# Two attention layers in one fixed order for four engines, value matmuls in query halves, 45 score tiles' exponentials on VectorE

## Chip, core and metric

The kernel runs on one core of a Trainium2 chip. The metric is device time in microseconds. The engines are called PE (TensorE), DVE (VectorE), ACT (ScalarE), POOL (GpSimd) and SP (SyncE, which issues DMAs).

## What is computed

Four layers run one after the other on x of 2048 tokens by 512 channels, 32 heads of 16: softmax attention (A), linear attention with a learned feature map (B), A and B again, each behind a layer norm and with a residual. The weights of both A layers are the same, and so are those of both B layers.

```python
def _A_ref(x, wqkv, wo):
    ...
    scores = jnp.einsum("bhqd,bhkd->bhqk", q, k) * (Dh ** -0.5)
    p = _softmax(scores, axis=-1)
    o = jnp.einsum("bhqk,bhkd->bhqd", p, v)
    return (lambda x, *d: x.transpose(*d))(o, 0, 2, 1, 3).reshape(B, S, D) @ wo
...
x = A_x
x = x + _A_ref(_layernorm(x, axis=-1), A_wqkv, A_wo)
x = x + _B_ref(_layernorm(x, axis=-1), B_wqkv, B_w_phi, B_wo)
x = x + _A_ref(_layernorm(x, axis=-1), A_wqkv, A_wo)
x = x + _B_ref(_layernorm(x, axis=-1), B_wqkv, B_w_phi, B_wo)
```

Matmul operands that are not FP32 are split into a high and a low FP16 part, so a projection is three passes.

## The kernel before

`LayerA.attention` is what the change rewrites. A layer's 32 heads are four octets `o` of eight heads. An octet has two groups `g` of four heads, and each group runs over four query blocks `j` of 512 and 16 key tiles `kt` of 128: 8 x 4 x 16 = 512 steps `n` a layer. A step has two score tiles (`half` 0 and 1, two heads each). `scores` (L944) computes one: eight matmuls into a PSUM tile `s` of 128 keys by 2 x 512 queries (there are two such tiles, four banks in all), then one ACT instruction that writes the exponentials to a tile `p` in SBUF (there are six). A row of `kq`, written with the shift, keeps the exponent in range, so no maximum is taken. `pvs` (L954) multiplies a step's two `p` tiles with the values `v`, FP32, eight matmuls of 512 columns, summed over the 16 key tiles in a PSUM pair `double`. After the last key tile `norm` (L554) turns the pair on DVE (`turned_sum`: two transposes `yt` on DVE, their sum on POOL), divides by the row sums on DVE, and with the second group of an octet `finish_o` writes the result `osp` and SP stores it to `oD`.

The rest of the layer is side work on PE between these, kept in the list `fill`. `octet(o)` projects the next octet's values (`pv`, turned like `yt` and stored in `v` by 16 DMAs, L726) and its queries and keys (`pqk`, L643); DVE scales and clamps them from PSUM into `stg` (`tq`, L821 to L826), POOL squares them, and SP loads `kq` from `stg` with 12 DMAs a group. `part(j)` multiplies three octets' output with `wo` (`po`) and DVE adds it to x (L626); `tail(j)` does the fourth and the next layer norm. In the first A layer `prep_b` folds `w_phi` into B's weights, and `prep_rest` loads the other weights, takes their largest element on DVE (`peaks`, L325) and splits them (`split_parts`, L145, L148). Side results go to a second PSUM pair, called by its use (`pv`, `pqk`, `po`, `psn`).

What sets the order: PE's is written by hand. The loop in `attention` puts half 1 of step n, then the value matmuls of step n - 1 or side work, then half 0 of step n + 1, and a credit of 1.45 to 1.75 side units a step says how much side work goes in:

```python
with tc.manual_schedule(engines={E.PE}):
    self.scores(*order[0], 0)
    for n, (g, j, kt) in enumerate(order):
        ...
        credit = min(credit + rate(n), 6)
        self.scores(g, j, kt, 1)
        turn = bool(pend) and pend[0][2] == 0 and not owed
        if turn:
            credit = sides(n, 3, credit, True)
        elif pend:
            self.pvs(*pend.popleft())
```

A pause of two or three steps (`GAP`, `hold`) after each side result is meant for DVE to empty the pair. The order on DVE, ACT and POOL is that of a list scheduler in the recording layer, which places instructions when the program is built. Each engine then runs its instructions in that order and waits on semaphores. SP's order comes from the same scheduler, before and after the change. The B layers and the stretch between layers are the same in both kernels but for line numbers, one added one-element operation where the shift is computed, and the place of a few rows where a layer ends.

## Time and profile before

| | us |
|---|---|
| three timed runs | 2669.97, 2670.04, 2676.82 |
| median | 2670.04 |
| the profiled execution | 2663.27 |
| its span, first to last instruction | 2661.4 |
| granted PE clock, mean | 0.974 |

The profile is one execution. A row of its groups names the source line, the engine, the operation and the tiles (out<-in), the shape and count, then busy time, the mean of one, and the idle time of the engine just before with what ended it. A row of the timeline has start and length in us and in brackets the idle time before it. Busy time counts overlapping instructions once. The lines that matter stand with the argument below.

### The profile page before, as it was taken

The numbers are of one execution on the slowest core, as the hardware profiler recorded it, in microseconds if no ns is written. First come the engines' busy times: TensorE is split into PE (matmuls) and PEld (weight loads), VectorE is DVE, ScalarE is ACT, GpSimd is POOL, SyncE is SP. The second block draws the span as 40 slices with busy tenths as digits, with TensorE's granted clock in tenths as the row PEclk, the third lists the DMA queues.
The fourth block names the chain that finished last, engine by engine and source line by source line (L and its number), as shares of the span: only waits on it lengthen the run. The fifth ranks groups of instructions, "written<-read, shape, count | busy, mean of one in ns | idle before, by whom it ended". The sixth has DMA issues, their size and how long they took to land.

```text
span 2661.4 us, 102775 instructions
## 1 busy us (share of the span) xinstructions
PE 2351.9 (88%) x46698; PEld 1100.2 (41%) x46698; DVE 1165.2 (44%) x2143; ACT 2194.4 (82%) x2426; POOL 486.5 (18%) x607
## 2 busy tenths in 40 slices
PE   7889998999888898899788899989998898888998
PEld 4444444444443343345344444444443344434543
DVE  8123222223333346599861233222232221557897
ACT  5899999999998798554438999999999899985453
POOL 3111110111100000266440111111111000004652
PEclk8999999999999999999899999999999999999999
DMA  5300320231035311000233003203300441110003
GB/s 197 70 13 7 56 38 3 40 66 35 18 78 142 141 69 66 17 25 1 76 101 53 15 7 51 39 3 49 61 3 11 94 118 50 58 58 21 13 17 105
DMA packets 111049, 138.62 MB, mean 52 GB/s; under 512 B 64025, under 2 KB 65673, under 8 KB 108425
## 3 DMA queue, kind: packets, MB, share of 16 engines
q1 hardware_dynamic: 109416, 129.18, 19.7%
q8 instruction: 367, 6.01, 0.9%
q0 software_dynamic: 1184, 2.77, 0.3%
q14 instruction: 82, 0.66, 0.1%
HBM read 60.06 MB, written 39.85 MB: 38 GB/s over the span
## 4 chain that ended last, share of the span: by engine, by line
ACT 47%; PE 18%; DVE 17%; issue 11%; POOL 3%; SPq 2%; DMA 1%; ACTq 0%; DVEq 0%; POOLq 0%
ACT p L951 45%; PE double L965 5%; PE s L948 3%; DVE su L1224 2%; DVE xt L626 1%; DVE yt L549 1%; POOL yt L550 1%; PE pbv L1154 1%; PE po L637 1%; PE pk L1154 1%; PE po L643 1%; SPq L726 1%; PE pq L1154 1%; POOL f L1233 1%; DVE st L432 1%
## 5 line engine op out<-in xcount | busy, mean ns | idle before, releaser
L951 ACT ACTIVATE p<-s 128x1024 f32<-128x1024 f32 x2048 | 1911.9, 1055 | 117.7 <-PE s L948 109.2
L965 PE MATMUL double<-p,v 64*32 64x512 f32 x16384 | 1117.9, 598 | 6.1 <-DVE yt L549 3.2
L948 PE MATMUL s<-kq 49*32 49x512 f16 x15488 | 828.5, 384 | 139.9 <-ACT p L951 112.9
L948 PEld LDWEIGHTS <-kq 49*32 49x32 f16 x15872 | 384.4, 90 | 898.9 <-issue 813.5
L965 PEld LDWEIGHTS double<-p,v 64*32 64x32 f32 x16384 | 320.6, 107 | 93.9 <-issue 30.4
L550 POOL TENSOR_TENSOR yt<-yt,yt 128x512 f32<-128x512 f32 x64 | 81.6, 1276 | 956.7 <-DVE yt L549 908.4
L549 DVE STREAM_TRANSPOSE yt<-double 128x512 f32<-128x512 f32 x128 | 84.2, 695 | 374.7 <-PE double L965 374.2
L821 DVE TENSOR_SCALAR tq<-pqk,c_qk 128x512 f32<-128x512 f32 x48 | 35.7, 744 | 342.6 <-PE pqk L643 330.0
L626 DVE SCALAR_TENSOR_TENSOR xt<-po,c_oA,xt 128x512 f32<-128x512 f32 x120 | 89.1, 743 | 219.9 <-PE po L643 214.3
L1154 PEld LDWEIGHTS <-xnTa 128*128 128x128 f16 x1152 | 111.2, 99 | 157.2 <-DVE f L1217 29.5
L744 POOL TENSOR_TENSOR sq<-stg 128x512 bf16<-128x512 f16 x48 | 58.2, 1212 | 498.9 <-DVE stg L823 389.7
L1233 POOL TENSOR_TENSOR f<-f,su 128x1024 f32<-128x1024 f32 x62 | 119.8, 1933 | 140.0 <-DVE su L1227 105.3
L549 DVE STREAM_TRANSPOSE vyt<-pv 128x512 f32<-128x512 f32 x48 | 31.9, 695 | 217.0 <-PE pv L643 216.7
L643 PE MATMUL po<-woA,ob 64*32 64x512 f16 x2304 | 100.2, 380 | 24.1 <-DVE xt L626 24.1
L1218 ACT ACTIVATE f<-f,c_pB 128x1024 f32<-128x1024 f32 x64 | 72.6, 1148 | 52.0 <-DVE f L1217 51.9
L1154 PE MATMUL pbv<-wbv,xnTa 128*128 128x512 f16 x384 | 93.1, 395 | 24.7 <-DVE f L1217 24.7
L643 PEld LDWEIGHTS <-wA 64*32 64x32 f16 x4608 | 77.7, 93 | 73.3 <-issue 39.6
L643 PE MATMUL pqk<-xnTb,wA 64*32 64x512 f16 x2304 | 96.4, 377 | 10.9 <-DVE tq L821 7.0
L643 PE MATMUL pqk<-xnT,wA 64*32 64x512 f16 x2304 | 95.1, 378 | 11.9 <-DVE tq L821 5.9
L1239 ACT ACTIVATE fk<-f 128x1024 f16<-128x1024 f32 x30 | 31.7, 1057 | 73.5 <-POOL f L1233 73.5
L1154 PE MATMUL pq<-wbqk,xnTa 128*128 128x512 f16 x384 | 88.4, 379 | 0.0
L1154 PE MATMUL pk<-wbqk,xnTa 128*128 128x512 f16 x384 | 88.1, 379 | 0.0
(262 smaller groups left out, 2241.1 us busy)
## 6 DMA issues: line engine op xcount, KB each, us to landing
kq<-stg SPq DMA_DIRECT2D x168, 128.0 KB
xd<-xt SPq DMA_DIRECT2D x40, 512.0 KB
xt<-xd SPq DMA_DIRECT2D x40, 512.0 KB
v<-vyt SPq DMA_DIRECT2D x384, 16.0 KB
oD<-osp SPq DMA_DIRECT2D x24, 256.0 KB
ob<-oD SPq DMA_DIRECT2D x8, 768.0 KB
xt<-in_A_x_dram SPq DMA_DIRECT2D x8, 512.0 KB
wbqk<-dBqk SPq DMA_DIRECT2D x2, 2048.0 KB
```

What stands on the lines that cost most here:

```text
L549: nc.vector.transpose(y.rearrange("p a b -> p (a b)"), half)
L550: nc.gpsimd.tensor_tensor(ys[0], ys[0], ys[1], ALU.add)
L626: nc.vector.scalar_tensor_tensor(xt[:, u, :], half, co, xt[:, u, :], op0=ALU.mult, op1=ALU.add)
L643: nc.tensor.matmul(ps[h][c, :], w[r, c], x[r], start=(n == 0), stop=(n == of - 1), skip_group_check=True)
L744: nc.gpsimd.tensor_tensor(sq, hi, hi, ALU.mult)
L948: nc.tensor.matmul(s[32 * c:32 * c + 32, u, :], self.side(g, half, 64 * u, 0, kt * P + 32 * c, 32), self.side(g, half, 64 * u, 1, j * 512, ...
L951: nc.scalar.activation(pt, s, AF.Exp, scale=0.25 / (QS * QS))
L965: nc.tensor.matmul(acc[h][32 * hh:32 * hh + 32, :], self.oct[o]["v"][r, x:x + 32], pt[r, hh % 2, :], start=(kt == 0), stop=(kt == NT - 1), ...
L1154: nc.tensor.matmul(dst, xnT[:, a, c, t * P:(t + 1) * P], w(b, c), start=(i == 0 and c == 0), stop=(i == 2 and c == NC4 - 1))
L1218: nc.scalar.activation(f, f, AF.Exp, scale=con["pB"])
L1224: nc.vector.tensor_reduce(su, f[:, r, :], AX.X, ALU.add)
L1233: nc.gpsimd.tensor_tensor(f3, f3, self.part_sums(f3, slice(0, 64), factor), ALU.mult)
```

## The change

`manual_schedule` in `attention` now covers PE, DVE, ACT and POOL. A planner inside the kernel's own build code (`Plan`, `streams`, the new loop) keeps a clock for PE, ACT, DVE and POOL from constants and writes every instruction of the attention in the order that this plan gives. Score tiles are placed when the plan says that their PSUM tile is free, value matmuls and side units where they fit before the next. Side work asks for a PSUM pair (`take`) only when the plan has it emptied; on DVE, emptying a pair has rank 0, ordinary work 1, the DVE exponentials 2, and the preparation of later weights 3. `LAND` lets 36 planned microseconds pass between a weight's load and its first reduction.

Value matmuls are issued in two halves of 256 queries (`pvs` with `part`). For up to one score tile in each of a layer's first 24 groups, the second half of the last key tile, PE writes the scores to a side pair and `power_task` computes the exponential on DVE, with one product a half on POOL: 23 tiles in the first A layer and 22 in the second. Scores are now scaled to a power of two by `ROOT` and `EXPS`, with a lift in the shift row. `finish_o` in attention became part of `norm_task`, with the low part's subtraction on POOL, not DVE. The folded B weights pass through DRAM (`dF`). `v_block`, which changes too, is in a branch for out-of-range inputs that does not run here.

Its core:

```diff
-LAG = 1
 STEPS = 2 * NJ * NT
-FILLED = 116
-
-FREE = -1
+FILLED = 112
+
 GAP = -2
+FAR = 1e9
+UNIT = 0.22
+PVHALF = 0.434
+EXP = 0.904
+THERE = 0.541
+BACK = 1.135
+POWERS = 24
+AHEADS = 0
+LATE = 0.08
+BACKGROUND = 100
...
     def split_parts(w, sc, name, *drams):
 
-        hl = big([P, 2, NC4, 512], F16, name)
+        hl = None
         for d in range(NC4):
-            split((hl[:, 0, d], hl[:, 1, d]), w[:, d], sc)
-            yield FREE
+            yield "V", 0.88, 3
+            if d == 0:
+                hl = big([P, 2, NC4, 512], F16, name)
+            nc.vector.tensor_scalar(hl[:, 0, d], w[:, d], sc, None, op0=ALU.mult)
+            yield "V", 0.75, 3
+            nc.vector.scalar_tensor_tensor(hl[:, 1, d], w[:, d], sc, hl[:, 0, d], op0=ALU.mult, op1=ALU.subtract)
...
+        def emptied(self, idx, ps, fn, cost):
+
+            for u in range(2):
+                yield "V", cost, 0
+                fn(idx, ps, u)
+            self.freed(idx)
...
+        def cols(self, n, of, w, x):
+
+            yield "M",
+            idx, ps = self.take()
+            for i in range(of):
+                yield "pe", UNIT
+                mm_cols(ps, w(i), x(i), i, of)
+            return idx, ps
...
+        def kq_task(self, o, j, ten, idx, ps, sqs):
+
...
+            yield "V", 0.75, 0
+            tq = np_.tile([P, 512], F32, tag="yt", name="tq", bufs=3)
+            nc.vector.tensor_scalar(tq, ps[0], cqk, None, op0=ALU.mult)
+            yield "V", 0.75, 0
+            nc.vector.scalar_tensor_tensor(tq, ps[1], cqk, tq, op0=ALU.mult, op1=ALU.add)
+            self.freed(idx)
+            yield "V", 0.43
+            nc.vector.tensor_scalar(hi, tq, CLAMP, -CLAMP, op0=ALU.min, op1=ALU.max)
...
+            yield "P", 1.28
+            nc.gpsimd.tensor_tensor(dst[:, 1], yb, dst[:, 0], ALU.subtract)
...
-        def scores(self, g, j, kt, half):
-            s = psS.tile([P, 2, 512], F32, tag="S", name="s")
+        def score_cols(self, g, j, kt, half, banks2):
             for c in range(4):
                 for u in range(2):
-                    nc.tensor.matmul(s[32 * c:32 * c + 32, u, :], self.side(g, half, 64 * u, 0, kt * P + 32 * c, 32),
+                    nc.tensor.matmul(banks2[u][32 * c:32 * c + 32, :], self.side(g, half, 64 * u, 0, kt * P + 32 * c, 32),
                                      self.side(g, half, 64 * u, 1, j * 512, 512), start=True, stop=True, skip_group_check=True)
+
+        def scores(self, G, kt, half):
+            s = psS.tile([P, 2, 512], F32, tag="S", name="s")
+            self.score_cols(*self.groups[G], kt, half, [s[:, u, :] for u in range(2)])
             pt = pp.tile([P, 2, 512], F32, tag="p", name="p")
-            nc.scalar.activation(pt, s, AF.Exp, scale=0.25 / (QS * QS))
-            self.pt[(g, j, kt, half)] = pt
-
-        def pvs(self, g, j, kt):
...
+        def power_task(self, G, kt, half, idx, ps):
+
+            pt = pp.tile([P, 2, 512], F32, tag="px", name="px", bufs=1)
+            new = lambda name: xp.tile([P, 512], F32, tag="xn", name=name, bufs=4)
+            ws = []
+            for u in range(2):
+                y = pt[:, u, :]
+                yield "V", 0.7, 0
+                nc.vector.tensor_scalar(y, ps[u], OFF, MAGIC, op0=ALU.add, op1=ALU.add)
+                yield "V", 0.7, 0
+                ws.append(new("pw"))
+                nc.vector.scalar_tensor_tensor(ws[u], y, MAGIC, ps[u], op0=ALU.subtract, op1=ALU.subtract)
+            self.freed(idx)
+            for u in range(2):
+                y, w = pt[:, u, :], ws[u]
+                yi = y.bitcast(I32)
+                yield "V", 0.4, 2
+                nc.vector.tensor_scalar(yi, yi, 23, PLEAD, op0=ALU.logical_shift_left, op1=ALU.bitwise_or)
+                yield "P", 1.0
+                z = new("pz")
+                nc.gpsimd.tensor_tensor(z, w, w, ALU.mult)
+                yield "V", 0.68, 2
+                nc.vector.scalar_tensor_tensor(y, z, PB, y, op0=ALU.add, op1=ALU.mult)
+                yield "V", 0.68, 2
+                nc.vector.scalar_tensor_tensor(z, w, PC, z, op0=ALU.mult, op1=ALU.add)
+                yield "V", 0.68, 2
+                nc.vector.scalar_tensor_tensor(y, z, PD, y, op0=ALU.add, op1=ALU.mult)
+                yield "V", 0.68, 2
+                nc.vector.scalar_tensor_tensor(y, w, PR, y, op0=ALU.add, op1=ALU.mult)
+            self.pt[(G, kt, half)] = pt
+            self.done[(G, kt, half)] = self.plan.end + 0.15
+
+        def pvs(self, G, kt, part, acc):
+            g, j = self.groups[G]
             o, par = g // 2, g % 2
-            if kt == 0:
-                pair = double()
-                self.acc = [pair[:, h, :] for h in range(2)]
-            acc = self.acc
+            f = slice(256 * part, 256 * part + 256)
             for hh in range(4):
-                pt = self.pt[(g, j, kt, hh // 2)]
+                pt = self.pt[(G, kt, hh // 2)]
                 x = kt * 132 + hh * 33 + 17 * par
                 for h in range(2):
                     r = slice(64 * h, 64 * h + 64)
-                    nc.tensor.matmul(acc[h][32 * hh:32 * hh + 32, :], self.oct[o]["v"][r, x:x + 32],
-                                     pt[r, hh % 2, :], start=(kt == 0), stop=(kt == NT - 1), skip_group_check=True)
-            del self.pt[(g, j, kt, 0)], self.pt[(g, j, kt, 1)]
...
+                    nc.tensor.matmul(acc[h][32 * hh:32 * hh + 32, f], self.oct[o]["v"][r, x:x + 32],
+                                     pt[r, hh % 2, f], start=(kt == 0 and part == 0), stop=(kt == NT - 1), skip_group_check=True)
...
+            with tc.manual_schedule(engines=COMPUTE):
+                while pvq or any(s.gens for s in self.streams):
+                    plan.now = pe
+                    plan.advance(pe)
...
+                    if tiles:
+                        free = estart[-2] + BACK if len(estart) > 1 else 0.0
+                        due = act - THERE
+                        if not slots:
+                            free = due = FAR
+                        if free <= pe:
+                            G, kt, h = tiles.popleft()
+                            if kt == NT - 1 and h == 1 and tried >= G:
+                                continue
...
+                            self.scores(G, kt, h)
+                            slots.sort()
+                            start = max(act, pe + THERE, slots.pop(0))
+                            lost += start - act
+                            act = start + EXP
+                            estart.append(start)
+                            self.done[(G, kt, h)] = start + BACK
+                            pe += UNIT
...
+                    first = need is not None and need[1][0] == "pe" and (ready <= AHEADS or len(need[1]) > 2 and ready <= 3)
+                    for turn in range(2):
+                        if first == (turn == 0):
+                            if need is not None:
+                                s, (kind, *what) = need
+                                if kind == "M":
+                                    soon = pvq and pvq[0][1] == NT - 1 or pvq and pvq[0][0] not in acc
+                                    if min(self.pfree) <= pe and not soon:
+                                        s.need, s.holds = None, True
+                                        break
+                                elif pe + what[0] <= max(due, free):
+                                    plan.now = pe + what[0]
+                                    s.need = None
+                                    pe += what[0]
+                                    self.stream_need(s)
+                                    break
+                        elif ready:
+                            G, kt, q = pvq[0]
+                            if (G in acc or min(self.pfree) <= pe) and pe + PVHALF <= max(due, free) + (LATE if ready > 1 else 0.0):
+                                if G not in acc:
+                                    acc[G] = self.take()
+                                pvq.popleft()
+                                idx, banks2 = acc[G]
+                                self.pvs(G, kt, q, banks2)
+                                pe += PVHALF
+                                plan.now = pe
+                                if q:
+                                    for h in range(2):
+                                        if not (kt == NT - 1 and h == 1 and tried >= G):
+                                            slots.append(pe + 0.35)
+                                        del self.pt[(G, kt, h)]
+                                    if kt == NT - 1:
+                                        pvdone = G + 1
+                                        self.spawn(self.norm_task(G, idx, banks2))
+                                break
+                        if turn == 0 and tiles:
+                            G, kt, h = tiles[0]
+                            if tried < G and G < POWERS and pvdone >= G and kt <= 9 and min(self.pfree) <= pe and G in acc and pe + UNIT <= max(due, free):
+                                tried = G
+                                npow += 1
+                                idx, ps = self.take()
+                                self.score_cols(*self.groups[G], NT - 1, 1, ps)
+                                pe += UNIT
+                                plan.now = pe
+                                self.spawn(self.power_task(G, NT - 1, 1, idx, ps))
+                                break
+                    else:
+                        pe = min(max(free, pe), pe + 0.02) if free > pe else pe + 0.02```

Three places in the orders of the two programs. First PE, in the first A layer while octet 1's keys are projected (`kqe` is the last part of the first group's keys and queries, `pqk` and `pm` are side banks). Before:

```order
L643 MATMUL pqk_3708<-xnT_1_153,wA 32x512
L643 LDWEIGHTS wA
L643 MATMUL pqk_3709<-xnT_1_153,wA 32x512
L948 LDWEIGHTS kqe
L948 MATMUL s<-kqe 32x512
```

and, eight score matmuls later,

```order
L948 LDWEIGHTS kqe
L948 MATMUL s<-kqe 32x512
L965 MATMUL double<-p,v_160 32x512 x8
L948 LDWEIGHTS kqe
L948 MATMUL s<-kqe 32x512
```

Now, at the same place:

```order
L1151 LDWEIGHTS kqe
L1151 MATMUL s<-kqe 32x512
L1202 MATMUL double<-p,v_162 32x256 x8
L685 LDWEIGHTS wA
L685 MATMUL pm_4227<-xnT_1_155,wA 32x512
```

Side work stood in runs of up to three groups of eight with whole value groups elsewhere; now a score group is followed by half a value group and one side group.

Second DVE, in the same layer where a query block ends (`yt` are the turned sums, `tq` and `stg` the keys and queries, `px`, `pw`, `pz` belong to an exponential on DVE). Before:

```order
L549 STREAM_TRANSPOSE yt_3845<-double 128x512
L549 STREAM_TRANSPOSE yt_3846<-double 128x512
L556 TENSOR_SCALAR rec<-yt_3845 128x16
L557 RECIPROCAL rec<-rec 128x16
L561 TENSOR_TENSOR yn<-yt_3845,rec 128x16x16
L821 TENSOR_SCALAR tq<-pqk_3708,c_qk 128x512
L822 SCALAR_TENSOR_TENSOR tq<-pqk_3709,c_qk,tq 128x512
```

Now:

```order
L850 STREAM_TRANSPOSE yt_3644<-double 128x512
L850 STREAM_TRANSPOSE yt_3670<-double 128x512
L873 TENSOR_SCALAR tq<-pm_3379,c_qk 128x512
L875 SCALAR_TENSOR_TENSOR tq<-pm_3380,c_qk,tq 128x512
L878 TENSOR_SCALAR stg<-tq 128x512
L921 TENSOR_SCALAR rec<-yt_3644 128x16
L881 TENSOR_SCALAR tq<-tq 128x512
L923 RECIPROCAL rec<-rec 128x16
L1169 TENSOR_SCALAR px<-pm_3735 128x512
L928 TENSOR_TENSOR yn<-yt_3644,rec 128x16x16
L1172 SCALAR_TENSOR_TENSOR pw<-px,pm_3735 128x512
```

The evacuation of the side pair moved ahead of `rec`, which waits for POOL's sum; the first operations on a side pair of scores follow.

Third DVE, near the end of the first A layer, at the reductions over the weight `bwo`. Before:

```order
L148 SCALAR_TENSOR_TENSOR bhlv<-bwv,sBv_sc,bhlv 128x512 x2
L626 SCALAR_TENSOR_TENSOR xt<-po_18460,c_oA,xt 128x512
L325 TENSOR_REDUCE pk_20294<-bwo 128x1
L626 SCALAR_TENSOR_TENSOR xt<-po_18461,c_oA,xt 128x512
L325 TENSOR_REDUCE pk_20296<-bwo 128x1
```

Now:

```order
L923 RECIPROCAL rec<-rec 128x16
L928 TENSOR_TENSOR yn<-yt_24453,rec 128x16x16
L936 STREAM_TRANSPOSE yb<-yn 128x512
L939 CAST osp<-yb 128x512
L327 TENSOR_REDUCE pk_24672<-bwo 128x1
L327 TENSOR_REDUCE pk_24693<-bwo 128x1
```

The reductions left the middle of an evacuation and stand one query block later.

More of the change, by code (lines that the diff above doesn't have):

```diff
@@ L1030, in more, with side_need @@
-        def more(self, gen, after=0):
-            self.fill.append([gen, after])
+        def more(self, gen):
+            self.fill.append(gen)
+        def side_need(self):
+            held = None
+            for s in self.streams[::-1 if self.now >= BACKGROUND else 1]:
+                need = self.stream_need(s)
+                if need is None:
+                    continue
+                if s.holds:
+                    return s, need
+                held = held or (s, need)
+            if held and any(s.holds for s in self.streams):
+                return None
+            return held
@@ L1052, in attention @@
+            self.groups = [(g, j) for g in range(6) for j in range(NJ)] + [(g, j) for j in range(NJ) for g in (6, 7)]
+            self.streams = [Task(), Task()]
+            for s, gens in zip(self.streams, (self.fill, deque())):
+                s.gens, s.need, s.holds = gens, None, False
+            self.plan, self.pfree, self.ready, self.now, self.last = Plan(), [0.0, 0.0], 0, 0, None
+            plan = self.plan
             for o in (1, 2, 3):
                 self.more(self.octet(o))
-            rest = iter(())
@@ L1110, in attention, with pairs @@
[L1110 removed]
+                self.streams[1].gens.append(extra[0])
+                plan.add(extra[1], 0.0)
+            def pairs(g):
+                self.alloc_pairs(g)
+                self.load_pairs(g)
+            events = []
+            for o in (1, 2, 3):
+                events.append((STEPS * o, lambda o=o: pvdone >= 8 * o or o < 3, lambda o=o: pairs(2 * o + 1)))
+                events.append((STEPS * o - STEPS + FILLED, lambda o=o: self.ready >= o, lambda o=o: pairs(2 * o)))
@@ L1111, in attention @@
+            assert not plan.tasks and not events
+            print("attention", self.li, "powers", npow, round(pe, 1), "exponentials", len(estart), "late", round(lost, 1), "ready", self.ready)
+            self.fill.append(self.last_tail(NJ - 1, self.last))
             state["att"], state["whole"] = False, True
-            while len(self.fill) > 1:
-                self.pumps(1)
             with tc.manual_schedule(engines=COMPUTE):
```

637 lines of the change are left out of this document (393 added, 244 removed).

## The prediction

> **What bounds the kernel now.** I read the page's busy line and chain first, then cut the span into its five stages.
>
> ```profile
> PE 2351.9 (88%) x46698; PEld 1100.2 (41%) x46698; DVE 1165.2 (44%) x2143; ACT 2194.4 (82%) x2426; POOL 486.5 (18%) x607
> ACT 47%; PE 18%; DVE 17%; issue 11%; POOL 3%; SPq 2%; DMA 1%; ACTq 0%; DVEq 0%; POOLq 0%
> 0.00:72.50 72.50, 51.19 (x378) 34.27 (x379) 59.01 (x149) 40.10 (x60) 25.69 (x58) 0.90 0.59 196
> 72.50:1096.50 1024.00, 912.63 (x21456) 414.92 (x21447) 338.95 (x659) 957.42 (x1024) 91.31 (x87) 0.98 0.23 54
> 1096.50:1407.90 311.40, 268.67 (x1944) 137.88 (x1941) 259.34 (x439) 134.26 (x177) 154.93 (x254) 0.95 0.15 47
> 1407.90:2409.10 1001.20, 896.95 (x21366) 404.53 (x21359) 291.17 (x550) 954.46 (x1024) 90.01 (x84) 0.99 0.20 44
> 2409.10:2661.40 252.30, 222.48 (x1576) 108.58 (x1572) 216.73 (x346) 108.11 (x141) 124.58 (x124) 0.96 0.12 41
> ```
>
> The columns are window, length, then busy us (and instructions) of PE, PEld, DVE, ACT, POOL, then the clock granted to PE, DMA share and GB/s. PE has the larger total, but the chain runs through ACT. Rows 2 and 4 are the two attention stages, 2025.2 us of the span; each holds 1024 ACT instructions, all exponentials. Everything the change does lies there. The other 636.2 us (72.5 + 311.4 + 252.3) keep their work.
>
> What should one exponential cost? Where scores are always ready the row is:
>
> ```profile
> 274.60:290.20 15.60, 15.60 (x18) 1.00 0.79 93
> 177.68 185.33 ACT L951 ACTIVATE p<-s 128x1024 f32<-128x1024 f32 x199 [1.04 <-PE s L948]
> L951 ACT ACTIVATE p<-s 128x1024 f32<-128x1024 f32 x2048 | 1911.9, 1055 | 117.7 <-PE s L948 109.2 <-ACT p L951 0.3
> ```
>
> The first row starts 17 instructions after its first one, so the pace is 15.60 / 17 = 0.917 us; the 1055 ns in the third row is the time of one from start to end, and neighbours overlap. 2048 x 0.917 = 1878.0 us. The stages take 2025.2, so **147 us** are lost: 85 in the first, 62 in the second. Of these the third row shows 117.7 us as plain idle time, nearly all "until PE's scores".
>
> Why are scores late? PE is in order and a wait for a PSUM bank stops the scores behind it. One of the larger stops, line by line (start, us, engine, line):
>
> ```profile
> 169.81 0.63 PE L643 MATMUL pqk<-xnT,wA 64*32 64x512 f16 x16
> 170.51 0.41 PE L948 MATMUL s<-kqe,kq 49*32 49x512 f16 x8
> 171.87 0.17 DVE L556 TENSOR_SCALAR rec<-yt 128x16 f32<-128x16 f32 x1 [1.44 <-POOL yt L550]
> 172.77 0.75 DVE L821 TENSOR_SCALAR tq<-pqk,c_qk 128x512 f32<-128x512 f32 x1
> 173.57 0.37 PE L643 MATMUL pqk<-xnT,wA 64*32 64x512 f16 x1 [2.65 <-DVE tq L821]
> 174.46 1.03 PE L948 MATMUL s<-kqe,kq 49*32 49x512 f16 x8
> 174.86 2.33 PE L965 MATMUL double<-p,v 64*32 64x512 f32 x16
> 175.34 1.41 DVE L826 TENSOR_TENSOR stg<-tq,stg 128x512 f16<-128x512 f32 x1
> 175.61 1.02 ACT L951 ACTIVATE p<-s 128x1024 f32<-128x1024 f32 x1 [3.32 <-PE s L948]
> ```
>
> DVE waits 1.44 us for POOL before `rec`, and the evacuation of pqk (L821) stands behind it. PE waits 2.65 us for the bank, ACT then 3.32 us. The scheduler's order of DVE made this, not a lack of DVE time. The largest single stop has another engine behind DVE:
>
> ```profile
> 877.24 5.47 SPq L409 DMA_DIRECT2D bwo<-in_B_wo_dram  x11
> 884.01 0.69 DVE L325 TENSOR_REDUCE pk<-bwo 128x1 f32<-128x512 f32 x1 [6.51 <-DMA bwo<-in_B_wo_dram]
> 885.41 1.05 PE L643 MATMUL po<-woA,ob 64*32 64x512 f16 x15 [7.48 <-DVE xt L626]
> 887.00 1.02 ACT L951 ACTIVATE p<-s 128x1024 f32<-128x1024 f32 x1 [8.84 <-PE s L948]
> ```
>
> A reduction that waits for a DMA sits between the two halves of an evacuation. After each stop the clock adds to the loss:
>
> ```profile
> 168.00:171.50 3.50, 2.85 (x80) 1.10 (x65) 1.31 (x2) 3.50 (x5) 0.93 (x1) 1.00 0.00 0
> 174.40:177.80 3.40, 3.36 (x48) 1.71 (x55) 2.26 (x3) 1.14 (x2) 1.19 (x1) 0.57 0.00 0
> ```
>
> The granted clock goes from 1.00 to 0.57, and the 16 value matmuls at 174.86 take 2.33 us. The Trainium skill (TensorE: Matmul & The Clock Gate, "What's actually happening") says that PE's clock drops to one half after an idle activity window of about 3.4 us and returns after a busy one; the trace agrees here. By that rule stops too short to make an idle window leave the clock at 1.00, and the loss that I leave in the sum below would shrink to that of rival 2, 2482; by the rows alone it stays.
>
> **The change part by part.** *Exponentials.* 1001 + 1002 remain on ACT. 45 x 0.917 = 41.3 us leave ACT; the floor is 2003 x 0.917 = 1836.8 us.
>
> *The 45 tiles on DVE.* Each has two halves of 512 columns: two operations that read PSUM, one shift and four operations with two SBUF inputs, and on POOL one product.
>
> ```profile
> L821 DVE TENSOR_SCALAR tq<-pqk,c_qk 128x512 f32<-128x512 f32 x48 | 35.7, 744 | 342.6 <-PE pqk L643 330.0 <-DMA v<-vyt 12.6
> L823 DVE TENSOR_SCALAR stg<-tq 128x512 f16<-128x512 f32 x48 | 20.3, 423 | 1.6
> 454.57 0.69 DVE L826 TENSOR_TENSOR stg<-tq,stg 128x512 f16<-128x512 f32 x1
> 175.01 1.19 POOL L744 TENSOR_TENSOR sq<-stg 128x512 bf16<-128x512 f16 x1 [3.18 <-DVE stg L823]
> L574 DVE TENSOR_TENSOR osp<-yb,osp 128x512 f16<-128x512 f32 x32 | 22.1, 690 | 0.9
> L550 POOL TENSOR_TENSOR yt<-yt,yt 128x512 f32<-128x512 f32 x64 | 81.6, 1276 | 956.7 <-DVE yt L549 908.4 <-DVE sBv_m L130 33.6 <-issue 14.4
> ```
>
> 4 x 0.744 + 2 x 0.423 + 8 x 0.690 = 9.3 us a tile on DVE, about 23 x 9.3 = 214 us a stage. With the 339 that DVE has in the first stage that is 553 of some 940 us: hidden, as long as evacuations go first, which the new order does. The operation itself is not in the trace. Below, its two-input operations could be as cheap as L823 (0.423: 7.2 us a tile); above, as dear as L826 at 175.34, which took 1.41 beside the POOL product of 175.01 where the one at 454.57 took 0.69: 4 x 0.744 + 0.846 + 8 x 1.41 = 15.1 us a tile, 347 a stage, 686 of 940, still hidden. I take 9.3. POOL gets 2 x 1.28 a tile, 59 us a stage on top of 91: hidden. The score matmuls of these tiles stay on PE and write the side banks.
>
> *Value matmuls in halves.* PE now issues 256 columns at a time. Rates from a full stretch:
>
> ```profile
> 199.74 0.84 PE L643 MATMUL pqk<-xnT,wA 64*32 64x512 f16 x24
> 200.38 0.41 PE L948 MATMUL s<-kqe 49*32 49x512 f16 x8
> 200.60 1.05 PE L965 MATMUL double<-p,v 64*32 64x512 f32 x16
> 201.47 0.41 PE L948 MATMUL s<-kq 49*32 49x512 f16 x8
> ```
>
> From start to start: three side groups 0.64 (0.213 each), a score group 0.22, a whole value group 0.87. A half by columns is 0.435. It was never run; the upper end is 0.87, if the number of instructions set the price. I take 0.435, because a score group loads as many weights and issues as many matmuls in 0.22 us, which is what one of a half's two rounds of eight must do. What the halves buy is order: in the changed program most score groups (508 of 1001 in the first stage) are followed by one half and one side group, 0.22 + 0.435 + 0.213 = 0.868 us, under the 0.917 of ACT. Before, a whole value group could stand between scores (0.22 + 0.87 = 1.09). PE's sum for a stage is 1001 x 0.22 + 1024 x 0.435 + 612 x 0.213 = 796 plus some 25 of transposes and DVE tiles: 821 of 918, so ACT stays the bound, with 10% to spare.
>
> *The fixed order.* Evacuations rank first on DVE, reductions over loaded weights stand last and some 36 planned us behind their load, and the product of `dst` moves from DVE to POOL. So the two stops above go. What is late next? PE asks for a bank pair 139 and 130 times a stage, each time as soon as the plan says it is empty; small lateness of DVE will show there. The best row for that is the 199 exponentials at 177.68, with side work and no long stop inside: 185.33 - 199 x 0.917 = 2.8 us lost. Scaled to 1002 that is 14 us a stage; I take **15**. The bounds are 0 and what is lost today, 73.6 a stage.
>
> *Queues, weight folding, shift constants.* The folded weights now go through DRAM (four stores, two loads) and the head has one more one-element DVE operation. Loads of kq start four key tiles earlier. All lie beside more than 900 us of ACT work; in the head it is under 0.4 us. Cost 0; without cover, a load of one tile like bwo above costs its 6.5 us.
>
> **The sum** against the profiled execution (2661.4 of span, 1.9 around it, 2663.3): 636.2 + 1836.8 + 30 + 1.9 = 2504.9, that is 158.4 less. The median of the runs is 2670.0, 6.8 above the profiled one; I keep that distance: 2670.0 - 158.4 = **2512**.
>
> **Rivals.** (1) *Half of the stops stay*: the chip strays from the plan, and in-order engines wait elsewhere. 37 a stage in place of 15: 2512 + 44 = 2556. For it: four engines are now in fixed order, so any late DMA holds them; against it: the two kinds of stop shown are order alone. (2) *No loss*: 2512 - 30 = 2482. For it: the period of 0.868 leaves 0.05 us of PE a tile to recover. (3) *Halves cost more.* At 0.50 the common period is 0.933, 0.016 over, on some 1030 periods: 17 us, 2529. At 0.60 PE needs 821 + 169 = 990 a stage and becomes the bound: 2 x 990 + 638 = 2618, 2625 on the median's scale. Nothing in the score rows speaks for that. (4) *Slower: DVE is late at every bank change.* The place is the first side matmul after a take. PE can lose about 0.25 us there unseen: 0.05 of the period, and some 0.2 from the second score buffer (an estimate: two exponentials take 1.83, of which a buffer is held 1.06 by its exponential, 0.41 by its scores, the rest partly by hand-overs). Each two-input operation caught beside POOL makes DVE 0.72 late (1.41 - 0.69). The gain of 158 is gone when 269 takes lose 0.59 each beyond 0.25, so from 0.84 us on; two caught operations before every take, 1.44, give 269 x 1.19 = 320 more, 2832. Against it: these operations rank behind evacuations, and POOL is busy a sixth of the stage (91 + 59 of 940). The Trainium skill (SBUF — State Buffer, "Who interferes with whom") states the rule behind it: a DVE instruction with two SBUF inputs and a GpSimd instruction that reads SBUF exclude each other for the whole instruction. Pairs like L826's agree; by it every two-input operation that meets POOL costs the 1.41, and whether that reaches PE is this rival. (5) *The gain does not show*: the same time comes back at the stage's end as side work left over. In the changed order one pair of transposed tiles is all that stands behind the last score of the first stage, and none in the second, so this is 2 us unless the plan's clock is wrong.
>
> **How the numbers follow.** Forecast (2490 to 2535) 0.56; no loss (2470 to 2490) 0.12; half of the stops (2535 to 2585) 0.17; halves or leftovers beyond 2585, yet faster, 0.06; same 0.03; slower 0.06. A measurement of this kernel tells 0.3% from no change, 8 us. So faster 0.91, same 0.03, slower 0.06; 2470 to 2585 holds 0.85.
>
> **What would show it.** Right: attention stages of about 933 us each, the idle time before the exponentials under 40 us in all, the granted clock near 1.00 in the stages, value rows of 256 columns in groups 0.43 to 0.45 apart, DVE near 60% there. Wrong: PE waiting over 1 us for DVE px or POOL pz again and again (rival 4), value groups over 0.5 apart (rival 3), or stages outside attention longer by more than 5 us.

## The result, and the profile after

| | before | after |
|---|---|---|
| runs, us | 2668.03 to 2676.82 (4) | 2605.12, 2606.65, 2600.37, 2613.33 |
| median, us | 2670.01 | 2605.89 |
| ratio, 95% interval | | 0.9757 [0.9727, 0.9787] |

The kernel is 64 us faster. The forecast was 158 faster, 2512, with a range that ended at 2585. Repeated later beside other kernels (`e11_after_again` below), the changed kernel took 2608.6 us.

The page of the changed kernel, busy line, chain and the queue of instruction fetches (packets, MB, share of the DMA engines):

```profile
PE 2377.6 (91%) x63082; PEld 1380.2 (53%) x63082; DVE 1559.6 (60%) x2745; ACT 2135.1 (82%) x2381; POOL 635.7 (24%) x735
ACT 46%; PE 24%; DVE 12%; issue 12%; SPq 3%; POOL 2%; DMA 1%; ACTq 0%; POOLq 0%; DVEq 0%
q8 instruction: 495, 8.11, 1.3%
```

PE has 16384 more matmuls and as many more weight loads than before. The five stages of the changed kernel, in the columns of the prediction's windows:

```profile
0.00:70.60 70.60, 49.08 (x371) 33.69 (x371) 57.81 (x144) 40.16 (x61) 24.58 (x52) 0.93 0.57 193
70.60:1056.90 986.30, 917.99 (x29601) 554.36 (x29607) 535.65 (x959) 926.27 (x1001) 164.93 (x157) 0.98 0.26 62
1056.90:1376.70 319.80, 274.48 (x1996) 140.86 (x1981) 266.56 (x456) 134.28 (x177) 156.72 (x253) 0.94 0.15 48
1376.70:2351.80 975.10, 911.92 (x29536) 541.57 (x29535) 483.33 (x843) 926.03 (x1002) 163.30 (x148) 0.98 0.22 46
2351.80:2603.30 251.50, 224.15 (x1588) 109.70 (x1588) 216.22 (x345) 108.32 (x141) 126.20 (x125) 0.96 0.12 41
```

Rows 2 and 4 are the attention stages: 986 and 975 us in place of the 933 forecast. ACT still waits for scores about as long as before, by the page's group:

```profile
L1158 ACT ACTIVATE p<-s 128x1024 f32<-128x1024 f32 x2003 | 1852.3, 1106 | 111.3 <-PE s L1151 108.4
```

The waits of PE in the changed kernel (us in total, times, longest) say for what:

```profile
PE pm L1202 <- issue: 19.9, 19, 2.6
PE pm L1151 <- DMA kqe<-sh: 14.0, 4, 7.5
PE pm L685 <- DMA ob<-oD: 13.4, 2, 9.8
PE s L1151 <- issue: 12.8, 11, 2.5
PE double L1202 <- issue: 5.9, 5, 2.2
PE double L685 <- issue: 4.3, 5, 1.6
```

In the same list of before, these rows concern the attention:

```profile
PE s L948 <- ACT p L951: 116.3, 334, 0.7
PE po L643 <- DVE xt L626: 30.0, 27, 7.5
PE pqk L643 <- DVE tq L821: 12.9, 7, 2.7
```

The first row is PE waiting for ACT, 334 times and never over 0.7 us: PE was early. Below it DVE's evacuations stood highest. After the change PE waits nowhere for an `xt` of the attention, and 2.2 us in all for `tq`. Two other kinds of wait stand there instead. The first is for data. The timeline of the changed kernel at its two largest stops:

```profile
81.53 0.60 PE L1151 MATMUL pm<-kq,kqe 49*32 49x512 f16 x1 [7.46 <-DMA kqe<-sh]
83.95 1.02 ACT L1158 ACTIVATE p<-s 128x1024 f32<-128x1024 f32 x1 [9.59 <-PE s L1151]
...
775.41 0.42 SPq L1209 DMA_DIRECT2D ob<-oD  x1
784.97 0.63 PE L685 MATMUL pm<-woA,ob 64*32 64x512 f16 x8 [9.78 <-DMA ob<-oD]
786.16 1.02 ACT L1158 ACTIVATE p<-s 128x1024 f32<-128x1024 f32 x1 [10.03 <-PE s L1151]
```

The planner let the first group's DVE tile ask for key tile 15 at the stage's start, when its keys `kqe` were still on their way, and let `part(0)` use `ob` as soon as SP was told to load it. PE is in order, so the scores behind waited too. The second layer has both stops again, smaller.

The second kind, "issue", has no releaser at all. PE stops in the middle of a value group:

```profile
889.04 0.64 PE L1202 MATMUL pm<-p,v 64*32 64x256 f32 x8
892.27 0.42 PE L1202 MATMUL pm<-p,v 64*32 64x256 f32 x4 [2.60 <-issue]
893.44 1.02 ACT L1158 ACTIVATE p<-s 128x1024 f32<-128x1024 f32 x1 [2.90 <-PE s L1151]
```

To weigh the kinds I took every exponential's start-to-start time less 0.917. Each lateness was put to what the profile names as the end of most of PE's idle time in it and in the 0.9 us before, if that idle time was over 0.4 of the lateness; the name is that of the matmul which ends the idle time. My own sum from the traces' instructions, us over both stages:

| kernel | late in all | PE "issue" | DMA | the rest |
|---|---|---|---|---|
| before | 146.7 | 0.3 | 0.1 | 146.3 |
| after | 123.9 | 62.2 | 31.0 | 30.7 |

### The profile page after: what moved, and what is told of

It reads as the page before. It is cut to its first block, busy times and chain, and to the rows that moved or that the text cites. A ratio compares the mean times of both kernels' runs of the same rounds, so it can differ in the third digit from the quotient of the medians.

```text
span 2603.3 us, 136308 instructions
## 1 busy us (share of the span) xinstructions
PE 2377.6 (91%) x63082; PEld 1380.2 (53%) x63082; DVE 1559.6 (60%) x2745; ACT 2135.1 (82%) x2381; POOL 635.7 (24%) x735
## 3 DMA queue, kind: packets, MB, share of 16 engines
q8 instruction: 495, 8.11, 1.3%
## 4 chain that ended last, share of the span: by engine, by line
ACT 46%; PE 24%; DVE 12%; issue 12%; SPq 3%; POOL 2%; DMA 1%; ACTq 0%; POOLq 0%; DVEq 0%
ACT p L1158 44%; PE s L1151 5%; PE pm L1202 4%; PE double L1202 3%; PE double L685 2%; PE pbv L1496 1%; DVE su L1566 1%; PE pk L1496 1%; PE po L668 1%; PE pm L685 1%; PE pq L1496 1%; SPq L863 1%; POOL f L1575 1%; DVE f L1558 1%; DVE st L474 1%
## 5 line engine op out<-in xcount | busy, mean ns | idle before, releaser
L1158 ACT ACTIVATE p<-s 128x1024 f32<-128x1024 f32 x2003 | 1852.3, 1106 | 111.3 <-PE s L1151 108.4
L1151 PE MATMUL s<-kq 49*32 49x512 f16 x15192 | 860.0, 386 | 63.3 <-ACT p L1158 17.4
L1202 PE MATMUL pm<-p,v 64*32 64x256 f32 x16592 | 693.1, 378 | 20.2 <-issue 19.9
L1151 PEld LDWEIGHTS <-kq 49*32 49x32 f16 x15872 | 392.7, 90 | 545.5 <-issue 407.5
L1202 PE MATMUL double<-p,v 64*32 64x256 f32 x15456 | 638.8, 380 | 3.7 <-issue 3.7
L1202 PEld LDWEIGHTS pm<-p,v 64*32 64x32 f32 x16592 | 349.0, 106 | 92.0 <-issue 34.7
L1202 PEld LDWEIGHTS double<-p,v 64*32 64x32 f32 x15456 | 320.8, 107 | 67.7 <-issue 14.1
L1235 DVE SCALAR_TENSOR_TENSOR xt<-double,c_oA,xt 128x512 f32<-128x512 f32 x78 | 58.1, 746 | 163.7 <-PE double L685 162.6
L850 DVE STREAM_TRANSPOSE yt<-pm 128x512 f32<-128x512 f32 x66 | 43.7, 696 | 159.2 <-PE pm L1202 159.0
L850 DVE STREAM_TRANSPOSE yt<-double 128x512 f32<-128x512 f32 x62 | 41.2, 696 | 159.8 <-PE double L1202 159.8
L1181 POOL TENSOR_TENSOR pz<-pw 128x512 f32<-128x512 f32 x90 | 103.5, 1151 | 128.3 <-DVE pw L1172 87.5
L685 PE MATMUL double<-woA,ob 64*32 64x512 f16 x2088 | 123.4, 378 | 1.7 <-issue 1.6
L685 PEld LDWEIGHTS <-wA 64*32 64x32 f16 x4608 | 86.4, 92 | 39.9 <-issue 2.7
L1183 DVE SCALAR_TENSOR_TENSOR px<-pz,px 128x512 f32<-128x512 f32 x90 | 82.2, 913 | 36.0 <-POOL pz L1181 28.6
```

Source lines behind the costliest of these rows:

```text
L685: nc.tensor.matmul(ps[h][c, :], w[r, c], x[r], start=(n == 0), stop=(n == of - 1), skip_group_check=True)
L850: nc.vector.transpose(ys[u].rearrange("p a b -> p (a b)"), ps[u])
L1151: nc.tensor.matmul(banks2[u][32 * c:32 * c + 32, :], self.side(g, half, 64 * u, 0, kt * P + 32 * c, 32), self.side(g, half, 64 * u, 1, j * ...
L1158: nc.scalar.activation(pt, s, AF.Exp, scale=EXPS)
L1181: nc.gpsimd.tensor_tensor(z, w, w, ALU.mult)
L1183: nc.vector.scalar_tensor_tensor(y, z, PB, y, op0=ALU.add, op1=ALU.mult)
```

## Experiments

Theory A: "issue" is PE waiting for its own instructions. Queue q8 moved 495 packets for 126164 PE instructions (255 each), before 367 for 93396 (254 each): PE's instructions come in blocks of 256. All 38 "issue" stops of PE over 0.35 us in after end at one and the same place in such a block; before has none. Rival, theory B: the plan is loose, such stops come from the order, and what is taken away comes back elsewhere.

**e1_waits.** The waits for data and one for the out-of-range test are taken away.

```diff
-if tried < G and G < POWERS and ...
+if tried < G and 0 < G < POWERS and ...
+            if j == 0:
+                yield "n", 356        # part(0)
+    with tc.manual_schedule(engines=COMPUTE):   # around lowest .. flag
```

> The kernel after, with three waits taken away: no DVE exponential in a layer's first group (so no score needs the late part kqe early), part 0 of the output side work starts at step 356 (8 steps after the loads of woA and ob are issued), and the out-of-range check stands behind the attention's instructions. Two more tiles go to ACT (2 x 0.917 = 1.8 us). Theory A (each large stop has a cause of its own, and the time behind a DMA wait is simply lost): the stops of 9.7, 7.3, 10.3, 3.7 and 3.9 us go, 34.9 in all, less 1.8: 2606 - 33 = 2573 us. Theory B (the plan is loose, in-order engines meet the next late thing instead): 2595 to 2610, with the loss of the two attention stages still near 125 us.

2599.17 us, 0.9729 [0.971, 0.9748]: B. The stages lose 121.4 us, near the 125 that B named. The trace shows why. `kqe` is gone (17 us), `ob` only in the second layer (in the first, step 356 was past before the weights allowed the load), and the test stayed in its place. With another order in the first group, DVE met two new waits for `v`'s DMAs, behind which ACT lost 5.6 and 3.8 us:

```profile
139.61 1.31 DVE L850 STREAM_TRANSPOSE yt<-double 128x512 f32<-128x512 f32 x2 [11.43 <-DMA v<-vyt]
140.98 1.96 PE L1202 MATMUL double<-p,v 64*32 64x256 f32 x32 [4.15 <-DVE yt L850]
...
150.34 0.75 DVE L873 TENSOR_SCALAR tq<-pm,c_qk 128x512 f32<-128x512 f32 x1 [7.12 <-DMA v<-vyt]
```

**e2_whole.** Value groups whole.

```diff
-            f = slice(256 * part, 256 * part + 256)
+            f = slice(0, 512)
-PVHALF = 0.434
+PVHALF = 0.868
-LATE = 0.08
+LATE = 0.3
-pvq = deque(... for q in range(2))
+pvq = deque(... for q in (1,))
```

> The kernel after, with value matmuls whole (512 columns, planned at 0.868 us and allowed to be 0.3 us late), so PE has about as many instructions as before. The planner's own time for the stages is then 960 and 953 us, against 920 and 913 with halves: 80 us more. Theory A (PE stops with no releaser are waits for PE's own instructions, of which the halves need 58 for each exponential and whole groups 42): those stops, 62 us of lateness in the two stages of after, fall under 10, and the time is 2606 + 80 - 55 = 2631 us. Theory B (these stops come from something else in the order, the number of instructions is innocent): the stops stay near 60 us and the time is about 2686.

2619.05 us, 0.9813 [0.9797, 0.9829]: A, and 12 better than it said. "Issue" lateness fell from 62.2 to 8.2 us, under the 10 that A named; the rest rose from 30.7 to 111, the price of the coarser order. So halves do buy the order that the prediction said, some 80 us, and give 54 of them back.

**e3_fewer_loads.** Three of seven `kq` loads a layer left out.

```diff
-events.append((STEPS * o, ..., lambda o=o: pairs(2 * o + 1)))
+events.append((STEPS * o, ..., lambda o=o: self.kq.__setitem__(2 * o + 1, self.kq[2 * o])))
```

> The kernel after; the groups 3, 5 and 7 of each layer use the loaded keys and queries of the group before, so three of the seven loads of kq in each layer are left out (results of these heads are other heads' results). Theory A (PE's instruction blocks are fetched late when kq is loaded at the same time; about 40 of the 62 us of PE stops without a releaser lie beside such loads): half of these 40 us go, 2606 - 20 = 2586 us. Theory B (the loads do not matter to PE): 2600 to 2612, and as many such stops as in after, 42 longer than 0.3 us.

2581.7 us, 0.9675 [0.9659, 0.9691]: A. "Issue" lateness is 40.3 us, 22 less, while DMA waits (30.9) and the rest (30.4) stayed as in after. In after, a fetch packet starts 0.9 us (median) after PE has entered the block before when DMA is idle, and 2.0 us when over 150 KB have moved in the last 1.5 us. Ahead of the stops over 0.35 us it starts 2.9 us after (median): there the fetch itself is late.

**e4_before_halves.** Halves alone, in the order of before.

```diff
-            for hh in range(4):
+            for f, hh in [(slice(x, x + 256), hh) for x in (0, 256) for hh in range(4)]:
...
-acc[h][32 * hh:32 * hh + 32, :], ..., pt[r, hh % 2, :], start=(kt == 0)
+acc[h][32 * hh:32 * hh + 32, f], ..., pt[r, hh % 2, f], start=(kt == 0 and f.start == 0)
```

> The kernel before, each value group issued as two sets of eight matmuls of 256 columns one right behind the other: the same work and the same order, 16 more matmuls and 16 more weight loads a step. Theory A (the number of PE instructions matters, since blocks of 256 arrive no faster than about one in 3.2 us, more slowly beside DMAs): PE stops without a releaser appear, some 20 to 50 us over the two stages, 2690 to 2720 us. Theory B (halves cost their columns and nothing else): 2670 within 8 us, and no such stops beyond the 9 us of before.

2705.37 us, ratio 1.0137 [1.0117, 1.0158]: A. With the same work in the same PE order the halves cost 35 us, and "issue" lateness went from 0.3 to 46.5 us. All 26 of its "issue" stops over 0.35 us end at the same place in a block. The page has the fetches of after:

```profile
PE 2380.3 (88%) x63082; PEld 1368.4 (51%) x63082; DVE 1164.5 (43%) x2143; ACT 2198.8 (81%) x2426; POOL 487.2 (18%) x607
q8 instruction: 495, 8.11, 1.3%
```

**e5_waits_again.** The waits of e1 once more, by other means.

```diff
+ and (G or kt >= 8)                  # the DVE tile of the first group
+            elif j == 0:
+                yield "gap", 12.0     # part(0), behind the loads
-    lowest = sp.tile([32, 1], F32, name="lowest", bufs=1)
+    lowest = sp.tile([P, H], F32, name="mx")[0:32, 0:1]
```

> The kernel after with the same three waits taken away in other ways: the DVE exponential of a layer's first group is tried only from key tile 8 on (when kqe has landed), part 0 starts 12 planned us after the loads of woA and ob are issued, and the out-of-range check uses a buffer that the last layer also uses, so it stands behind the attention. The tiles on ACT stay 2003. Theory A (time behind a DMA wait is lost time, and taking the wait away returns it): 9.7 + 7.3 + 10.3 + 3.7 + 3.9 = 34.9 us less, 2571 us. Theory B (what e1_waits showed: the order shifts, and other DMA or DVE waits take the place): 2590 to 2606.

2592.49 us, 0.9708 [0.9676, 0.974]: inside B's range, but not for B's reason. The stages took 977.5 and 958.1 us, 25.7 less than after, most of A's 34.9; but the last stretch took 263.1, 11.6 more. There PE waits for `wbo`. SP reads the test's flag in order, and now it reads it late, so the load behind it is late. The same in e8, described below: the reading of the flag (its start, 2504.3 us, stands twice), then SP's load and PE:

```profile
L1807 SPq TENSOR_LOAD <-flag x1: 489/489/489, 2504.3 to 2504.3; - x1
2505.24 0.34 SPq L689 DMA_DIRECT2D wbo<-dBo  x1
2510.09 7.12 PE L657 MATMUL po<-wbo,obB 128*128 128x512 f16 x24 [11.81 <-DMA wbo<-dBo]
```

**e6_no_dve_tiles.** `POWERS = 0`.

> The kernel after with no exponential on DVE: all 2048 tiles go to ACT. The planner's own time is 932.8 and 931.8 us (920.0 and 912.9 with them). Theory A (ACT sets the pace between the stops, and the 45 tiles are worth 45 x 0.917 = 41.3 us; the wait for kqe, 17 us, belongs to a DVE tile and goes too): 2606 + 41 - 17 = 2630 us. Theory B (PE sets the pace, and the DVE tiles, whose scores PE computes all the same, are worth little): 2590 to 2606.

2625.36 us, 0.9835 [0.9801, 0.9868]: A. The 45 tiles are worth 19.5 us net (24.4 in the stages), since they also brought the `kqe` wait.

**e7_quarters.** Still more instructions for the same columns.

```diff
-            f = slice(256 * part, 256 * part + 256)
-            for hh in range(4):
+            for f, hh in [(slice(x, x + 128), hh) for x in (256 * part, 256 * part + 128) for hh in range(4)]:
```

> The kernel after, each half of a value group issued as two sets of 128 columns in place of one of 256: the same columns, 91 PE instructions for each exponential in place of 59. Theory A (a block of 256 PE instructions takes at least some 3.2 to 3.4 us to fetch, and PE waits when it uses one faster): 91.1 / 256 x 3.3 = 1.17 us for each exponential, 2003 x 1.17 + 642 outside the stages = 2990 us, with PE stops of 0.5 to 1 us without a releaser at every block. Theory B (the number of instructions is innocent): 2606 within 15 us. Theory C (PE is slower at each short matmul, not at the fetch): as long as A, but PE busy in the time added, without stops at every 256th instruction.

3435.37 us (one run): A's mechanism, 445 above its number, since a block took 3.90 us in the mean, not the 3.3 I had put. The page of the quarters:

```profile
PE 2519.1 (73%) x95850; PEld 1878.5 (55%) x95850; DVE 1561.5 (45%) x2745; ACT 2206.5 (64%) x2381; POOL 635.4 (19%) x735
PE 56%; issue 25%; DVE 8%; ACT 8%; POOL 2%; SPq 1%; DMA 0%; ACTq 0%; POOLq 0%; DVEq 0%
q8 instruction: 751, 12.30, 1.5%
```

And its waits of PE:

```profile
PE pm L1201 <- issue: 289.3, 243, 4.1
PE double L1201 <- issue: 268.7, 234, 4.0
PE s L1151 <- issue: 112.2, 104, 3.6
```

PE is busy 142 us longer than in after, so theory C explains at most that of the 830 us added. All 650 "issue" stops of PE over 0.35 us end at the same place in a block. Time from one block's first instruction to the next one's, in the stages, from the traces:

```
kernel    blocks   1% are under   median   mean
before       334       3.94       5.61    6.06 us
after        462       3.47       3.95    4.25
quarters     716       3.45       3.74    3.90
```

Three kernels with quite different work meet one floor or stay above it: with whole groups no block comes near 3.47, with halves a part does, with quarters most. 716 blocks at 3.47 are 2485 of the 2791 us of its two stages (1407.1 + 1384.1); the rest is in blocks that took longer.

**e8_whole_in_places.** e5 with whole groups where side work is dense.

```diff
+whole = q == 0 and any(a <= self.now < b for a, b in ((0, 16), (96, 152), (224, 280), (368, 416)))
+cost, late = (2 * PVHALF, 0.3 if ready > 2 else 0.0) if whole else (PVHALF, LATE if ready > 1 else 0.0)
-... pe + PVHALF <= max(due, free) + (LATE if ready > 1 else 0.0):
+... pe + cost <= max(due, free) + late:
```

> e5_waits_again, with whole value groups (512 columns) at steps 0 to 16, 96 to 152, 224 to 280 and 368 to 416 of each layer, where after has most of its PE stops without a releaser (side work is dense there and kq is loaded), and halves elsewhere. The planner's own time is 927.5 and 925.5 us, 20 more than with halves only. Theory A (fewer instructions there take most of the fetch stops away, some 40 of 62 us): 20 us less than e5_waits_again, about 2551. Theory B (no fetch stops saved, or as much lost by the coarser order): 5 to 20 us more than e5_waits_again.

2575.3 us, 0.9649 [0.9614, 0.9683]: 17 under e5, near the 20 of A, but at most half of it is A's. "Issue" lateness fell by 40 us, from 60.1 in e5 to 20.0, and the coarser order took most of that back: the rest rose from 33.5 to 62.6. In the profiled executions the stages are 9.6 us shorter than in e5. The stretch between the layers is also 9.6 shorter, and no run shows why.

**e9_check_left, e10_places_check_left, e11_after_again.** e5 and e8 with the test where it was, and after itself, on one chip. The edits of e9 and e10 hold one thing more, which their expectations do not name. It shortens a planned gap in the first attention layer, behind a load of B's weights:

```diff
-                yield "gap", 20.0
+                yield "gap", 12.0
```

No run has that edit alone, so what is put down to the test below holds only up to its effect.

> e5_waits_again with the out-of-range check where it stands in after; only the waits for kqe and ob are taken away. In e5's trace the stretch behind the second attention took 263.1 us against 251.5 in after, with POOL 5.9 us idle for the check's reduction there. Theory A (the time of e5 went into the moved check, and 31 us of DMA waits are worth what they measure where nothing else is late): 11 less at the end and up to 3.9 more in the second attention than e5: 2581 to 2586 us. Theory B (waits taken away come back as others whatever is done): 2592 or more, as e5 and e1.

> e8_whole_in_places with the out-of-range check where it stands in after. Theory A (the moved check costs e8 some 10 us at the end): 2565 to 2570 us. Theory B (it costs nothing): 2575.

> The kernel after, unchanged, for a comparison on the same chip: 2606 us within 5 by every theory.

e9 took 2589.1 us, 0.9714 [0.9695, 0.9732]; e10 2574.08, 0.9656 [0.9635, 0.9678]; after 2608.6, 0.9764 [0.9749, 0.978]. e9 lies between its two theories. In it `kqe` is gone, but 12.5 of the 14 us of `ob` waits are there again: 19.5 us under e11 for about 18 us of DMA waits less. e10 is B. Its last stretch is back at 250.6 us (e8: 261.3), but its stages are 7.3 us longer (PE waits 3.5 us where DVE stands behind the test, and 3.2 for `ob` in the second layer), so about nothing is left of the 5 to 10 expected. Of the kernels with right results e10 and e8 are the fastest, both below after with intervals apart. The stages of e10 in the windows' columns:

```profile
70.70:1044.50 973.80, 914.35 (x26864) 504.32 (x26864) 554.53 (x988) 928.60 (x1000) 168.20 (x159) 0.99 0.26 63
1357.10:2316.60 959.50, 898.94 (x26784) 492.94 (x26783) 495.75 (x857) 926.34 (x1001) 165.65 (x150) 0.99 0.22 47
```

And what is left there of PE's waits for instructions:

```profile
PE double L685 <- issue: 5.7, 5, 2.4
PE double L1202 <- issue: 3.9, 3, 1.7
PE pm L685 <- issue: 2.6, 3, 2.3
PE s L1151 <- issue: 2.3, 5, 1.0
```

All in one table, lateness as above:

| kernel | median, us | late in all | PE "issue" | DMA | rest |
|---|---|---|---|---|---|
| before | 2670.0 | 146.7 | 0.3 | 0.1 | 146.3 |
| after | 2605.9 | 123.9 | 62.2 | 31.0 | 30.7 |
| e1, waits | 2599.2 | 121.4 | 66.2 | 10.3 | 44.9 |
| e2, whole | 2619.1 | 145.4 | 8.2 | 25.7 | 111.4 |
| e3, fewer loads | 2581.7 | 101.7 | 40.3 | 30.9 | 30.4 |
| e4, before with halves | 2705.4 | 184.9 | 46.5 | 0 | 138.4 |
| e5, waits again | 2592.5 | 98.2 | 60.1 | 4.5 | 33.5 |
| e6, no DVE tiles | 2625.4 | 107.0 | 64.9 | 11.4 | 30.8 |
| e7, quarters | 3435.4 | 954.3 | 874.9 | 17.1 | 62.3 |
| e8, whole in places | 2575.3 | 90.5 | 20.0 | 7.8 | 62.6 |
| e9, test left | 2589.1 | 109.7 | 63.6 | 12.5 | 33.6 |
| e10, places, test left | 2574.1 | 97.8 | 20.9 | 10.0 | 66.9 |

## Why the prediction was wrong

**The step that failed** is the loss: "Scaled to 1002 that is 14 us a stage; I take 15." It measured 68.0 and 55.9. The row behind it came from before, where 41.9 PE instructions go with an exponential (42903 in 1024). After the change there are 59.1 (59208 in 1001), and the sum had no term for their supply. "If the number of instructions set the price" was weighed only for the array's time; there 0.435 was right, as the timeline of after shows:

```profile
92.91 0.41 PE L1151 MATMUL s<-kq 49*32 49x512 f16 x8
93.13 0.63 PE L1202 MATMUL double<-p,v 64*32 64x256 f32 x16
93.56 0.41 PE L685 MATMUL pm<-xnT,wAv 64*32 64x512 f16 x8
93.83 0.41 PE L1151 MATMUL s<-kq 49*32 49x512 f16 x8
```

The half takes 0.43 from start to start. But these 32 matmuls have 32 weight loads, 64 instructions in 0.92 us, a block in 3.68. Hardly a block came faster than 3.47. The 0.2 us between are less than what a busy DMA adds to a fetch (2.0 - 0.9 = 1.1), and then PE stops. By the table 62 us are lost so. Another 31 go to the waits for the loads of `kqe` and `ob`, a term that the sum had at "Cost 0": the loads were taken to be hidden beside ACT's work, and these two had a user too early in the fixed order.

The rest, 30.7, is as large as the 30 of the forecast, and that is luck in part. Only 9.2 of it stand behind waits of PE for DVE, which the 15 a stage were meant for. It also hangs on the pace: the median exponential of after starts 0.904 us after the one before it, and against 0.904 the loss would be 150 and the rest 56.

**The sum closes.** Loss 123.9 for 30: +93.9. Outside attention 641.9 for 636.2 (the stretch between the layers is 8.4 longer, the ends 2.7 shorter together): +5.7. The median stands 0.8 above the profiled run (2605.12), not 6.8: -6.0. 2512 + 93.6 = 2605.6, and 2605.9 was measured.

**Right:** that ACT's 2003 exponentials are the floor; that the evacuation stops would go (lateness behind waits for DVE fell from 83.6 to 9.2 us); that POOL and DVE would hide the DVE tiles (DVE was busy 54 and 50% of the stages, near 60 forecast). Two groups of DVE in after:

```profile
L1183 DVE SCALAR_TENSOR_TENSOR px<-pz,px 128x512 f32<-128x512 f32 x90 | 82.2, 913 | 36.0 <-POOL pz L1181 28.6 <-DVE px L1178 0.5
L1189 DVE SCALAR_TENSOR_TENSOR px<-pw,px 128x512 f32<-128x512 f32 x90 | 63.3, 704 | 2.9
```

Alone, both take 0.69 us, the value in the sum. 40 of the 90 of L1183 ran beside an instruction of POOL and took 1.19 (4 of L1189, 0.97). That is the effect of rival 4, but PE waited for these tiles once, 1.0 us. Of the 41.3 us they were to save, 19.5 showed (e6). The clock stood at 0.98 in both stages, not near 1.00. It dropped to half ten times there, 65 us in all. Ahead of five of these drops PE had no stop over 2.5 us and was busy for 0.35 to 0.47 of the 3.41 us before, so short stops did not leave the clock at 1.00, as the prediction had considered.

**Rivals.** Rival 1 was the nearest in kind ("any late DMA holds them"); it was given 0.17 and held 31 us of the 94. Rival 3 named the right part of the change with the wrong mechanism: its 2625 for halves 0.60 apart is the nearest time, by luck, since they stood 0.43 apart. Rivals 2 and 4 did not happen; of 5 there are at most the 4.2 us named next.

**Open:** the 8.4 us between the layers. With them the time outside attention grew by more than 5 us, one of the prediction's signs of being wrong. 4.2 of them stand there when B's third projection (`pbv`) starts, behind a pair of transposes that waits for the last layer norm; the rest was not traced, and the stretch lay between 309 and 321 us in the other runs. That a DMA delays a fetch by standing ahead of it in a DMA engine fits e3 but was not shown by itself.

## What to carry to other kernels

Count an engine's instructions per unit of the bound, not only its busy time: cutting one matmul in two is nearly free on the array and not in the supply of instructions, and "issue" stops at a fixed place in each 256 are the sign. Where density is near the limit, put fewer, larger instructions in the places where transfers run. In a fixed order, a load needs its own time in the plan before its first user on every engine, and a wait that is moved must be followed on every queue: a flag that SP reads in order held the load of a weight behind it.

## What the runs showed of the hardware

PE used its instructions in blocks of 256, and in every kernel with halves or quarters only 1% of the blocks took less than 3.45 to 3.47 us, 74 instructions a us (the shortest in after 3.38, in the quarters 2.90). In after, the packet itself took 1.07 us (median), and where PE had to wait it went on 2.4 us after the packet's start. In the quarters, where PE nearly always waits, the packet starts some 1.16 us after PE enters the block before, about 1.8 beside heavy DMA, and PE goes on 2.41 us later: 1.16 + 2.41 = 3.57 by these medians, close above the floor. The Trainium skill (Runtime: NRT & Kernel Launch, "Instruction fetch mechanics") describes blocks of 256 that are fetched while the one before runs, and calls the cost mostly hidden; the packets here agree with the blocks, and the 62 us show that it is not hidden where PE takes 64 instructions in 0.92 us.
